# Attention, dense MLP and routed experts on one core: a new order of the attention phase, another float64 decode, a hinted branch

## The chip, the cores and the metric

The kernel runs on one core of one Trainium2 chip. The metric is the device time of one execution in microseconds (us); the median over runs is compared.

## The reference

Three stages follow one another, each over all 1536 tokens (2 batches of 768):

1. Attention with 8 heads of 64: each query sees the keys of the last 96 positions and the first 8 ("global") keys, with a linear distance penalty by head; `n_global` and `n_local` are inputs.

```python
is_global = pos[None, :] < int(n_global)
is_local = (rel >= 0) & (rel < int(n_local))
scores = np.where(keep, scores + bias, -1e9); a = softmax(scores); x = a @ v
```

2. A dense MLP, 512 to 2048 to 512, whose weights `w_in`, `w_out` are float64: `h = x @ w_in; g = max(h, 0) + alpha * min(h, 0); x = g @ w_out`.

3. Eight experts with top-1 routing: `logits = x @ w_gate + modality_bias[modality_id]`, each token goes to its best expert, `relu(x @ w1[e]) @ w2[e]`, scaled by the softmax weight.

## The kernel before

**Precision and tiles.** Every fp32 matmul of the first two stages is three matmuls on values split into a high and a low part. Tokens are cut into 12 tiles of 128; for the MLP two tiles form a block of 256, so there are 6 blocks, and the 16 slices of 128 hidden features are worked in 4 groups of 4.

**Attention of one tile `ti`** (lines 515 to 662): `load_attn` loads `kr`, `qr`, `vr` (256 KB each); `attn_T` transposes k and q on TensorE and splits them into `ring` and `qT`; `attn_S` makes the scores in PSUM (`a`); `attn_P` adds the bias on VectorE (CUSTOM_DVE into `sp`, with the row minimum `mn`) and takes exp on ScalarE; `attn_PT` transposes the probabilities into `pth`; `attn_V` splits v on GpSimd into `vring`; `attn_PV` multiplies and normalises into `x`; `attn_X` transposes `x` into `xT`, the MLP's input.

**MLP step** (lines 1015 to 1053): `step_a` makes `h` (12 matmuls), then ScalarE, VectorE and GpSimd make `t` and the split `g`; `step_b` accumulates `g @ w_out` in `acc`. PSUM holds two banks of `h`.

**Decode of a weight slice** (lines 366 to 383): `load_w` brings 512 KB of raw float64 words (`wraw`); `decode_into` makes fp32 out of the high word `hw` and the top bits of the low word `lw`, into `dx`, and splits it into `w`. There are 32 decodes; the first 10 lie in the attention phase. Before, one decode is: ScalarE Abs; four VectorE instructions (clamp, mask and shift, merge sign, merge low bits); ScalarE Copy; GpSimd subtract.

**What sets the order.** While `plan.on`, instructions are only recorded. `Plan.issue` then simulates the engines with a table of costs and emits the recorded work in the order of simulated starts; among the instructions that could start within `slack` of the earliest, an engine takes the one of the lowest rank, slope times base plus offset by the table `URGENCY` (a kind has two letters at most: L loads of k and q, C constants, D decodes, and so on). There are two such plans: the first covers all of the attention, the first 10 decodes and the MLP steps of blocks 0 to 4 of feature group 0; the second the rest of the MLP up to its last group. The engines run each queue in order; SP issues nearly all loads.

**Between the plans** stands `wide_path` (line 1098): a path for general `n_global` and `n_local` behind a branch that is not taken here. It holds `dense_attention`, unrolled over 8 heads, and a redo of the MLP steps done so far. Every engine loads the flag `fli` (L1099) and branches (L1100); on the way around, each engine adds the semaphore counts that the path would have added and jumps to the join.

`more_constants` (line 476) makes the MLP's `alpha_sb` and the gate's `wg`, `mbs` and `thr`. Line 152 is the recorder, so all recorded instructions bear it, and line 70 is a helper's.

Of the kernel before, what the change touches and what calls it, by code (L numbers as in the profile page):

```python
# [10 lines left out]
F32 = mybir.dt.float32  # L11
# [4 lines left out]
U32 = mybir.dt.uint32  # L16
# [6 lines left out]
P = 128  # L23
# [8 lines left out]
URGENCY = {  # L32
# [6 lines left out]
}  # L39
SLACK = ((63.05, 1544.0), (185.8, math.inf))  # L40


class Plan:
# [9 lines left out]
    }  # L53
    ISSUE, TURN, FIRST, DONE = 500, 1230, 850, 1400

    def __init__(self, tc):
# [210 lines left out]

    def issue(self, rank, slack, ahead):

        self.on = False  # L270
        self.link()
        start = self.simulate(rank, slack, ahead)
        with self.tc.manual_schedule():
            for k in sorted(range(len(self.ops)), key=lambda k: (start[k], k)):
                for call in self.ops[k]["calls"]:
                    call()
        self.ops = []
# [3 lines left out]
def tile_kernel(  # L281
# [51 lines left out]
    def load_attn(ti):  # L333
        b, i = divmod(ti, TPB)
        r = []
        for src, nm in ((k, "kr"), (q, "qr"), (v, "vr")):
            plan.kind = (ti - 1.0, "LV" if nm == "vr" else "L")
            t = ap2.tile([P, H, D], F32, tag=nm, name=nm)
            Y.dma_start(out=t, in_=src[b, :, i * P:(i + 1) * P, :].rearrange("h p d -> p h d"))
            r.append(t)  # L340
        plan.kind = (-2.0, "C")
        raws[ti] = [r[1], r[0], r[2]]
# [23 lines left out]
    def decode_into(t, hi, lo):  # L366
        t = t.rearrange("p k f w -> p (k f) w")
        lw, hw = t[:, :, 0], t[:, :, 1]
        x = decp.tile([P, 512], F32, tag="dx", name="dx")
        S.activation(out=x, in_=hw.bitcast(F32), func=ACTF.Abs)  # L370
        V.tensor_scalar(out=x, in0=x, scalar1=CHI, scalar2=CLO, op0=ALU.min, op1=ALU.max)
        xu = x.bitcast(U32)
        V.tensor_scalar(out=xu, in0=xu, scalar1=0x07FFFFFF, scalar2=3, op0=ALU.bitwise_and, op1=ALU.logical_shift_left)
        V.scalar_tensor_tensor(out=xu, in0=hw, scalar=0xC0000000, in1=xu, op0=ALU.bitwise_and, op1=ALU.bitwise_or)
        V.scalar_tensor_tensor(out=xu, in0=lw, scalar=29, in1=xu, op0=ALU.logical_shift_right, op1=ALU.bitwise_or)
        S.activation(out=hi, in_=x, func=ACTF.Copy)
        G.tensor_tensor(out=lo, in0=x, in1=hi.bitcast(F32), op=ALU.subtract)
# [18 lines left out]
    plan.on = True  # L396
    plan.kind = (-2.0, "C")
    gl = const.tile([P, 4], U32, name="gl")
    Y.dma_start(out=gl[:, 0:2], in_=n_global.bitcast(U32).partition_broadcast(P))
    Y.dma_start(out=gl[:, 2:4], in_=n_local.bitcast(U32).partition_broadcast(P))  # L400
    load_attn(0)
    mraw = const.tile([NTT, P, 2], U32, name="mraw")
    plan.kind = (0.0, "CM")
    Y.dma_start(out=mraw, in_=mod_id.bitcast(U32).rearrange("(t p w) -> t p w", p=P, w=2))
    mrf = const.tile([NF, 2, P], F32, name="mrf")
# [69 lines left out]

    def more_constants():
        nonlocal alpha_sb, mbs, wg, thr
        G.memset(x2[:, :, DM:XW], 0.0)
        wg = const.tile([P, KD, 96], F32, name="wg")
# [8 lines left out]
        T.transpose(mtp[:, 64:64 + NF], mrf[:, 1], ident[0:NF, 0:NF])  # L488
        mf = const.tile([P, 2, NTT], F32, name="mf")
        V.tensor_copy(out=mf[:, 1], in_=mtp[:, 0:NTT])  # L490
        alpha_sb = const.tile([P, NF], F32, name="alpha_sb")
        V.tensor_scalar(out=alpha_sb, in0=mtp[:, 64:64 + NF], scalar1=-1.0, scalar2=1.0, op0=ALU.mult, op1=ALU.add)
# [207 lines left out]
    def dense_attention():  # L700
# [4 lines left out]
        xo = small[:, 400:400 + D]  # L705
        qb = small[:, 480:480 + D]
        vb = flat[:, 7 * SEQ:7 * SEQ + TPB * D].rearrange("p (t d) -> p t d", d=D)
        qt = flat[0:D, 7 * SEQ + TPB * D:7 * SEQ + TPB * D + P]
# [6 lines left out]
        HS = SEQ // 2  # L715
        for h in range(H):
            slope = 2.0 ** -(8.0 * (h + 1) / H)
            with tc.For_i(0, B, 1) as b:
                V.memset(qoff, 0.0)
                with tc.For_i(0, TPB, 1) as i:  # L720
                    for src, dst in ((k, kb), (v, vb)):
                        Y.dma_start(out=dst.unsqueeze(1), in_=src[ds(b, 1), h].rearrange("o (t p) d -> p o t d", p=P))
                    Y.dma_start(out=qb.unsqueeze(1), in_=q[ds(b, 1), h, ds(i * P, P)].rearrange("o p d -> p o d"))
                    pa, pb = bank(ps_a, "a"), bank(ps_a, "a")
# [17 lines left out]

                    V.scalar_tensor_tensor(out=r, in0=r, scalar=-slope, in1=s, op0=ALU.mult, op1=ALU.add)
                    V.tensor_scalar(out=s, in0=s, scalar1=nls[h], scalar2=None, op0=ALU.add)
                    V.tensor_tensor(out=s, in0=s, in1=t1, op=ALU.mult)
# [17 lines left out]
                    V.tensor_scalar(out=xo, in0=pa[:, 0:D], scalar1=sm_, scalar2=None, op0=ALU.mult)  # L763
                    Y.dma_start(out=xgen[ds(b * SEQ + i * P, P), h * D:(h + 1) * D], in_=xo)
                    V.tensor_scalar(out=qoff, in0=qoff, scalar1=float(P), scalar2=None, op0=ALU.add)

    with kind(3.0, "C3"):
        nlsl = const.tile([P, H], F32, name="nlsl")
        for h in range(H):
            V.tensor_scalar(out=nlsl[:, h:h + 1], in0=nl, scalar1=-(2.0 ** -(8.0 * (h + 1) / H)), scalar2=None, op0=ALU.mult)  # L770
    nls = [nlsl[:, h:h + 1] for h in range(H)]

# [319 lines left out]
    LAG = 2  # L1092

    def rank(base, name):
        slope, offset = URGENCY[name]
        return slope * base + offset

    def wide_path(done):
        wide = nc.values_load(fli[0:1, 0:1], min_val=0, max_val=1)  # L1099
        with tc.If(wide > 0, preferred_fallthrough_block=False):  # L1100
            dense_attention()
# [11 lines left out]
            V.memset(x2[:, :, DM:XW], 0.0)  # L1113

    for s_i in range(len(steps) + LAG):
        if s_i < len(steps):
            gi, b, f = steps[s_i]
            if gi == 0 and wp2 is None:
                while f == 0 and b < CB and next(tiles) < (b + 1) * BT - 1:
                    pass  # L1120
                if b == 0 and f == 0:
                    with kind(3.0, "C3"):
                        more_constants()
                if b >= CB and f == 0:
                    for _ in tiles:
                        pass
                    plan.issue(rank, *SLACK[0])
                    wide_path(s_i)
                    at.close()
                    wp2 = p1.enter_context(tc.tile_pool(name="wp2", bufs=GF + 2, side="right", reuse_waits="tile"))  # L1130
                    plan.on = True
            if gi == NF // GF - 1 and b == 0 and f == LAG:
                plan.issue(rank, *SLACK[1])
# [235 lines left out]
```

## Time and profile before

| | us |
|---|---|
| median of 3 runs (lowest, highest) | 608.0 (606.66, 609.71) |
| the profiled execution | 610.72 |
| its span, first to last instruction | 608.9 |
| TensorE matmul (PE) busy | 572.6 (94%) |
| TensorE weight load (PEld) busy | 512.9 (84%) |
| VectorE (DVE) busy | 374.7 (62%) |
| ScalarE (ACT) busy | 309.1 (51%) |
| GpSimd (POOL) busy | 211.0 (35%) |

Busy times are over the whole span, so they hide the stages. The attention phase with its MLP steps reaches from 0 to 162.2 us, where TensorE comes to the branch; the rest of the MLP to about 400; routing and experts to the end. TensorE's busy time is modelled and can hold short gaps. Of the clock that was granted to TensorE the page tells the level: 1.00 is full speed, 0.50 half.

### The profile page before, as it was taken

How to read it: one execution, taken by the hardware profiler on the slowest of the kernel's cores; microseconds unless marked ns; L12 is line 12 of the kernel's file. 1: busy time of each engine (PE TensorE's matmuls, PEld its weight loads, DVE VectorE, ACT ScalarE, POOL GpSimd, SP SyncE). 2: the span in 40 equal slices, each digit the busy share in tenths (PEclk: the TensorE clock that was granted, in tenths of full speed). 3: DMA queues.
4: the chain of work that ended last, by engine and by line, in shares of the span. 5: the costliest groups of instructions: out<-in, count | busy, mean ns of one | idle time of the engine just before them, and what ended most of it. 6: DMA issues, size and time to landing. Idle time of an engine off the chain costs nothing. (4 is left out here: it accounts for less than half of the span.)

```text
span 608.9 us, 13266 instructions
## 1 busy us (share of the span) xinstructions
PE 572.6 (94%) x4572; PEld 512.9 (84%) x4572; DVE 374.7 (62%) x979; ACT 309.1 (51%) x671; POOL 211.0 (35%) x239
## 2 busy tenths in 40 slices
PE   2889999999799999999999999998999999999995
PEld 2778888898688888989998999887889999998994
DVE  6899998686366787775222433878282269972221
ACT  5867887776355444543332333444372268862221
POOL 4835474442146554563322212213012112230110
PEclk9889999999989999999999999999999999999998
DMA  7854569946134332330000000463822399940120
GB/s 191 174 131 134 124 153 163 180 81 104 35 83 127 103 105 71 104 103 1 1 2 0 36 36 36 158 201 94 278 71 62 98 309 363 356 138 34 36 63 26
DMA packets 94384, 69.53 MB, mean 114 GB/s; under 512 B 61883, under 2 KB 82391, under 8 KB 94296
## 3 DMA queue, kind: packets, MB, share of 16 engines
q1 hardware_dynamic: 91736, 60.84, 37.0%
q0 software_dynamic: 2560, 7.64, 4.2%
q8 instruction: 40, 0.66, 0.5%
q14 instruction: 48, 0.39, 0.2%
HBM read 92.88 MB, written 7.30 MB: 165 GB/s over the span
## 5 line engine op out<-in xcount | busy, mean ns | idle before, releaser
L152 PE MATMUL acc<-w,g 128*128 128x512 f32 x432 | 111.1, 404 | 4.9 <-issue 3.9
L152 PE MATMUL h<-xT,w 128*128 128x256 f32 x888 | 114.7, 285 | 0.1
L152 PEld LDWEIGHTS h<-xT,w 128*128 128x128 f32 x888 | 110.8, 190 | 3.3 <-DVE t L152 0.5
L70 PE MATMUL h<-mw,xs 128*128 128x256 f32 x720 | 98.4, 285 | 1.3 <-DVEq L1300 0.7
L152 PEld LDWEIGHTS acc<-w,g 128*128 128x128 f32 x432 | 79.6, 192 | 22.2 <-issue 4.1
L70 PE MATMUL acc<-mw,ht 128*128 128x512 f32 x360 | 97.1, 407 | 0.5 <-DVEq L1300 0.5
L70 PEld LDWEIGHTS h<-mw,xs 128*128 128x128 f32 x720 | 91.3, 189 | 4.7 <-DVEq L1300 1.1
L152 POOL TENSOR_TENSOR g<-t,g 128x256 fp32r<-128x256 f32 x74 | 60.2, 817 | 92.2 <-ACT g L152 62.2
L70 PEld LDWEIGHTS acc<-mw,ht 128*128 128x128 f32 x360 | 63.5, 189 | 12.2 <-DVEq L1300 0.8
L70 POOL DMA_INDIRECT out<-y,sidx x15 | 18.4, 1225 | 146.2 <-DVE y L70 115.9
L152 DVE SCALAR_TENSOR_TENSOR t<-t,alpha_sb,h 128x256 f32<-128x256 f32 x74 | 35.2, 478 | 51.8 <-ACT t L152 49.2
L70 DVE TENSOR_TENSOR mw<-raw,mw 128x1024 fp32r<-128x1024 f32 x48 | 57.8, 1227 | 9.1 <-ACT mw L70 7.4
L152 POOL TENSOR_TENSOR w<-dx,w 128x512 fp32r<-128x512 f32 x32 | 43.4, 1359 | 44.7 <-ACT w L152 42.7
L70 ACT ACTIVATE hs<-h 128x256 f32<-128x256 f32 x60 | 22.9, 381 | 69.3 <-PE h L70 65.3
L152 ACT ACTIVATE t<-h 128x256 f32<-128x256 f32 x74 | 28.1, 380 | 51.9 <-PE h L152 50.4
L70 DVE TENSOR_TENSOR ht<-a,ht 128x256 fp32r<-128x256 f32 x60 | 25.3, 422 | 47.0 <-ACT ht L70 46.9
L70 ACT ACTIVATE mw<-raw 128x1024 fp32r<-128x1024 f32 x48 | 49.4, 1055 | 6.5 <-DMA raw<-in_moe_w 2.4
L152 DVE SCALAR_TENSOR_TENSOR dx<-wraw,dx 128x512 uint32<-128x512 uint32 x64 | 50.9, 799 | 0.5
L152 ACT ACTIVATE sp<-sp,mn 128x256 f32<-128x256 f32 (+1 forms) x96 | 39.8, 480 | 11.1 <-DVE mn L152 10.9
L152 ACT ACTIVATE g<-t 128x256 fp32r<-128x256 f32 x74 | 30.8, 417 | 26.7 <-DVE t L152 21.7
L70 POOL TENSOR_TENSOR g<-t,g 128x256 fp32r<-128x256 f32 x22 | 17.9, 815 | 58.6 <-ACT g L70 58.5
L70 PE MATMUL acc<-w,g 128*128 128x512 f32 x144 | 38.0, 400 | 0.0
(168 smaller groups left out, 851.9 us busy)
## 6 DMA issues: line engine op xcount, KB each, us to landing
raw<-in_moe_w SPq DMA_DIRECT2D x117, 512.0 KB
wraw<-in_moe_w_in SPq DMA_DIRECT2D x16, 512.0 KB
wraw<-in_moe_w_out SPq DMA_DIRECT2D x16, 512.0 KB
xs<-x SPq DMA_DIRECT2D x12, 258.0 KB
kr<-in_k SPq DMA_DIRECT2D x12, 256.0 KB
qr<-in_q SPq DMA_DIRECT2D x12, 256.0 KB
vr<-in_v SPq DMA_DIRECT2D x12, 256.0 KB
vring<-vglob SPq DMA_DIRECT2D x8, 96.5 KB
```

The costliest lines, as they stand in the source:

```text
L70: return method(*a, **kw)
L152: call = lambda: method(*a, **kw)
```

## The change

- **Start.** The kinds of tile 0's k and q get a rank below everything (base -1e6), the two scalars `gl` come next; `mraw` is no longer loaded among them.
- **Decode.** ScalarE takes Abs scaled by 65536 and, new, Sign in place over `hw`. The clamp and, new, the multiplication by the sign go to GpSimd in the first plan and to VectorE behind it. VectorE shifts `lw` in place and merges: in the first plan two instructions for four.
- **Constants.** `alpha_constants` stays in the first plan; `gate_constants` (`wg`, `mbs`, the modality's transpose, the memset of `x2`'s last columns) goes into the second.
- **Branch.** The flag is loaded inside the first plan, ahead of work whose simulated start lies within `LEAD` of the end, and TensorE gets a prefetch hint for the branch there. The general path now stands right behind the branch, with the way around last.
- **General attention** loops over heads in the program in place of 8 unrolled copies; the eight `nlsl` constants go. On ScalarE the rows between branch and join fall from about 180 to about 80.
- **Tables.** `URGENCY` and the first `SLACK` have new numbers, so all of the first plan is in a new order.

```diff
-    "A": (0.02, 228.0), "B": (0.06921, 81.0), "C": (16.99, -57.0), "C1": (17.59, 5.0),
+    "A": (95.73, -22.0), "B": (100.0, 46.0), "C": (0.7547, -17.0), "C1": (0.7079, -94.0),
...
-SLACK = ((63.05, 1544.0), (185.8, math.inf))
+SLACK = ((57.46, 1710.0), (185.8, math.inf))
...
+    LEAD = 8000
...
-    def issue(self, rank, slack, ahead):
+    def issue(self, rank, slack, ahead, late=None):
...
+                if late and start[k] > max(start) - self.LEAD:
+                    late()
+                    late = None
...
-            plan.kind = (ti - 1.0, "LV" if nm == "vr" else "L")
+            plan.kind = (ti - 1.0 if ti or nm == "vr" else -1e6, "LV" if nm == "vr" else "L")
...
+        eng = G if plan.on and wp2 is None else V
-        S.activation(out=x, in_=hw.bitcast(F32), func=ACTF.Abs)
-        V.tensor_scalar(out=x, in0=x, scalar1=CHI, scalar2=CLO, op0=ALU.min, op1=ALU.max)
+        S.activation(out=x, in_=hw.bitcast(F32), func=ACTF.Abs, scale=65536.0)
+        S.activation(out=hw.bitcast(F32), in_=hw.bitcast(F32), func=ACTF.Sign)
+        eng.tensor_scalar(out=x, in0=x, scalar1=CHI * 65536.0, scalar2=CLO * 65536.0, op0=ALU.min, op1=ALU.max)
         xu = x.bitcast(U32)
-        V.tensor_scalar(out=xu, in0=xu, scalar1=0x07FFFFFF, scalar2=3, op0=ALU.bitwise_and, op1=ALU.logical_shift_left)
-        V.scalar_tensor_tensor(out=xu, in0=hw, scalar=0xC0000000, in1=xu, op0=ALU.bitwise_and, op1=ALU.bitwise_or)
-        V.scalar_tensor_tensor(out=xu, in0=lw, scalar=29, in1=xu, op0=ALU.logical_shift_right, op1=ALU.bitwise_or)
+        V.tensor_scalar(out=lw, in0=lw, scalar1=29, scalar2=None, op0=ALU.logical_shift_right)
+        V.scalar_tensor_tensor(out=xu, in0=xu, scalar=3, in1=lw, op0=ALU.logical_shift_left, op1=ALU.bitwise_or)
+        eng.tensor_tensor(out=x, in0=x, in1=hw.bitcast(F32), op=ALU.mult)
         S.activation(out=hi, in_=x, func=ACTF.Copy)
         G.tensor_tensor(out=lo, in0=x, in1=hi.bitcast(F32), op=ALU.subtract)
...
-    plan.kind = (-2.0, "C")
+    plan.kind = (-5e5, "C")
     gl = const.tile([P, 4], U32, name="gl")
...
-        for h in range(H):
-            slope = 2.0 ** -(8.0 * (h + 1) / H)
+        with tc.For_i(0, H, 1) as h:
...
+    def wide_flag():
+        wide.append(nc.values_load(fli[0:1, 0:1], min_val=0, max_val=1))
+        tc.mark_branch_hint_location("wide", hint=wide[0], engines=EN_PE)
+
     def wide_path(done):
-        wide = nc.values_load(fli[0:1, 0:1], min_val=0, max_val=1)
-        with tc.If(wide > 0, preferred_fallthrough_block=False):
+        with tc.If(wide[0] > 0, label="wide"):
...
-                        more_constants()
+                        alpha_constants()
...
-                    plan.issue(rank, *SLACK[0])
+                    plan.issue(rank, *SLACK[0], wide_flag)
                     wide_path(s_i)
...
+                    with kind(40.0, "L2"):
+                        gate_constants()
```

The order of instructions at three places follows. First SP, which issues the loads, at the start of the program; before:

```order
L152 DMA gl<-in_n_global 128x2
L152 DMA gl<-in_n_local 128x2
L152 DMA wraw<-in_moe_w_in 128x4x256
L152 DMA wraw<-in_moe_w_out 128x1024
L152 DMA kr<-in_k 128x8x64
L152 DMA qr<-in_q 128x8x64
L152 DMA kr<-in_k 128x8x64
L152 DMA qr<-in_q 128x8x64
L152 DMA vr<-in_v 128x8x64
L1099 TENSOR_LOAD fli
```

and in the changed kernel:

```order
L154 DMA kr<-in_k 128x8x64
L154 DMA qr<-in_q 128x8x64
L154 DMA gl<-in_n_global 128x2
L154 DMA gl<-in_n_local 128x2
L154 DMA wraw<-in_moe_w_in 128x4x256
L154 DMA wraw<-in_moe_w_out 128x1024
L154 DMA mrf<-in_moe_alpha 16x128
L154 DMA vr<-in_v 128x8x64 x2
L154 DMA kr<-in_k 128x8x64
L154 DMA qr<-in_q 128x8x64
```

Tile 0's k and q went from behind two weight loads to the front; tile 1's went behind two loads of v; SP's load of the flag left this place.

Second, GpSimd (POOL) where the first weights are decoded, with tile numbers; before, behind the constants:

```order
L152 COPY fscr<-fscr 128x128
L152 TENSOR_TENSOR w_229<-dx,w_229 128x512
L152 TENSOR_SCALAR vring_126<-vr 128x8x64
L152 TENSOR_TENSOR vr<-vr,vring_126 128x512
L152 TENSOR_SCALAR vring_126<-vr 128x512
L152 TENSOR_TENSOR vring_126<-vr,vring_126 128x512
```

and in the changed kernel (`dx<-dx` is the clamp, `dx<-dx,wraw` the multiplication by the sign):

```order
L154 TENSOR_SCALAR dx<-dx 128x512
L154 COPY fscr<-fscr 128x32
L154 TENSOR_SCALAR vring_125<-vr 128x8x64
L154 COPY fscr<-fscr 128x128
L154 TENSOR_TENSOR vr<-vr,vring_125 128x512
L154 TENSOR_SCALAR vring_126<-vr 128x8x64
L154 TENSOR_SCALAR vring_125<-vr 128x512
...
L154 TENSOR_TENSOR dx<-dx,wraw 128x512
L154 TENSOR_TENSOR vring_126<-vr,vring_126 128x512
L154 TENSOR_TENSOR w_222<-dx,w_222 128x512
```

One GpSimd instruction of a decode became three, among the splits of v.

Third, TensorE (PE) in front of the branch; before:

```order
L152 MATMUL h<-xT,w_258 128x256 x12
L152 MATMUL a<-ident,x 128x128 x4
L1099 TENSOR_LOAD fli
L1100 COMPARE_AND_BRANCH
L1100 UNCONDITIONAL_BRANCH
```

and in the changed kernel (the left out rows are the last tile's `attn_PV`):

```order
L154 MATMUL h<-xT,w_240 128x256 x12
L1115 TENSOR_LOAD fli
L1385 BRANCH_PREFETCH_HINT
L154 MATMUL acc<-w_225,g 128x512 x6
L154 MATMUL h<-xT,w_251 128x256 x12
...
L154 MATMUL acc<-w_234,g 128x512 x6
L154 MATMUL a<-ident,x 128x128 x4
L1119 COMPARE_AND_BRANCH
```

The flag's load and the hint moved ahead of 24 MLP matmuls, `attn_PV` and the last transposes; the branch now stands right behind those transposes, whose copy is ScalarE's last work there too.

## Rows read from the trace of the kernel before

**Rows 1.** Busy us of each engine by stretch (instructions), clock, DMA share, GB/s.

```profile
core 0: us, PE busy (x) PEld busy (x) DVE busy (x) ACT busy (x) POOL busy (x), PEclk, DMA share, GB/s
0.00:20.00 20.00, 8.42 (x62) 6.81 (x63) 14.34 (x61) 12.58 (x33) 11.47 (x30) 1.00 0.85 187
20.00:100.00 80.00, 73.69 (x953) 65.38 (x948) 76.06 (x253) 61.57 (x133) 44.60 (x49) 0.96 0.62 138
100.00:162.00 62.00, 60.54 (x752) 53.42 (x750) 41.01 (x122) 39.36 (x85) 24.70 (x31) 1.00 0.69 122
166.00:380.00 214.00, 212.85 (x1358) 192.69 (x1359) 117.30 (x252) 89.49 (x210) 86.18 (x93) 0.99 0.18 58
```

**Rows 2.** Timeline of the start: start us, length us, instruction, idle time before.

```profile
1.29 0.42 SPq L152 DMA_DIRECT2D gl<-in_n_local  x1
...
5.53 0.24 DVE L152 TENSOR_SCALAR gparts<-gl 128x2 uint32<-128x2 uint32 x2 [1.49 <-DMA gl<-in_n_local]
...
10.10 1.09 PE L152 MATMUL a<-ident,kr 128*128 128x128 f32 x4 [10.10 <-DMA kr<-in_k]
...
15.01 0.29 DVE L152 CUSTOM_DVE_ANT_0 sp<-a,bias 128x128 f32<-128x128 f32 x1
...
16.18 1.11 PE L152 MATMUL a<-ident,kr 128*128 128x128 f32 x4
...
18.47 0.65 PE L152 MATMUL a<-ident,qr 128*128 128x128 f32 x4 [0.32 <-PE a L152]
```

**Rows 3.** The view of Rows 1, of four short stretches.

```profile
4.00:16.00 12.00, 5.09 (x32) 4.17 (x32) 9.15 (x48) 7.56 (x21) 4.39 (x8) 1.00 1.08 261
24.00:30.00 6.00, 5.85 (x72) 5.28 (x70) 5.16 (x21) 5.23 (x12) 3.97 (x6) 0.72 0.60 130
34.00:40.00 6.00, 4.79 (x65) 4.41 (x63) 5.69 (x23) 4.92 (x11) 1.82 (x3) 0.72 0.30 91
164.00:172.00 8.00, 5.90 (x15) 4.74 (x16) 4.03 (x8) 2.21 (x4) 0.03 (x1) 0.58 0.11 19
```

**Rows 4.** TensorE's waits, 20 to 100 us: total us, times, longest.

```profile
PE a L152 <- DVE pth L152: 1.8, 3, 1.2
PE a L152 <- DVE x L152: 1.4, 2, 1.2
```

**Rows 5.** Groups on VectorE, 20 to 100 us: the decodes (busy us, mean ns).

```profile
L152 DVE SCALAR_TENSOR_TENSOR dx<-wraw,dx 128x512 uint32<-128x512 uint32 x15 | 10.3, 684 | 0.1
...
L152 DVE TENSOR_SCALAR dx<-dx 128x512 f32<-128x512 f32 x8 | 4.4, 555 | 0.0
...
L152 DVE TENSOR_SCALAR dx<-dx 128x512 uint32<-128x512 uint32 x8 | 3.3, 418 | 0.0
```

**Rows 6.** Groups on GpSimd, 20 to 100 us, of the same size.

```profile
L152 POOL TENSOR_TENSOR w<-dx,w 128x512 fp32r<-128x512 f32 x8 | 10.9, 1361 | 21.7 <-ACT w L152 21.7
L152 POOL TENSOR_SCALAR vring<-vr 128x512 bf16<-128x512 f32 x15 | 10.4, 691 | 10.9 <-PE a L152 9.7 <-DMA vr<-in_v 0.6
```

**Rows 7.** Instructions that write `dx`, whole span: ns least/median/most.

```profile
L152 DVE TENSOR_SCALAR dx<-dx x64: 397/426/1131, 8.3 to 277.2; 128x512 f32<-128x512 f32 x32, 128x512 uint32<-128x512 uint32 x32
L152 DVE SCALAR_TENSOR_TENSOR dx<-wraw,dx x64: 649/687/1667, 9.3 to 280.8; 128x512 uint32<-128x512 uint32 x64
L152 ACT ACTIVATE dx<-wraw x32: 646/666/707, 7.4 to 274.3; 128x512 f32<-128x512 f32 x32
```

**Rows 8.** Timeline around the branch, columns as in Rows 2.

```profile
161.62 0.60 PE L152 MATMUL a<-ident,x 128*128 128x128 f32 x4
...
162.25 0.60 ACT L152 ACTIVATE xT<-a 128x512 fp32r<-128x512 f32 x1
...
166.10 1.22 PE L152 MATMUL acc<-w,g 128*128 128x512 f32 x2 [3.89 <-issue]
166.75 0.67 ACT L152 ACTIVATE dx<-wraw 128x512 f32<-128x512 f32 x1 [3.52 <-issue]
```

**Rows 9.** Instructions of the branch, line 1100: ns least/median/most, first to last start.

```profile
L1100 PEldq COMPARE_BRANCH  x2: 95/1866/3638, 161.8 to 162.4; - x2
```

More of the change, by code (lines that the diff above doesn't have):

```diff
@@ L400, in tile_kernel @@
     Y.dma_start(out=gl[:, 2:4], in_=n_local.bitcast(U32).partition_broadcast(P))
+    plan.kind = (-2.0, "C")
     load_attn(0)
-    mraw = const.tile([NTT, P, 2], U32, name="mraw")
     plan.kind = (0.0, "CM")
-    Y.dma_start(out=mraw, in_=mod_id.bitcast(U32).rearrange("(t p w) -> t p w", p=P, w=2))
     mrf = const.tile([NF, 2, P], F32, name="mrf")
@@ L474, in tile_kernel, with alpha_constants, gate_constants @@
     alpha_sb = mbs = wg = thr = None
-    def more_constants():
-        nonlocal alpha_sb, mbs, wg, thr
+    def alpha_constants():
+        nonlocal alpha_sb
+        mtp = bank(ps_a, "a")
+        T.transpose(mtp[:, 0:NF], mrf[:, 1], ident[0:NF, 0:NF])
+        alpha_sb = const.tile([P, NF], F32, name="alpha_sb")
+        V.tensor_scalar(out=alpha_sb, in0=mtp[:, 0:NF], scalar1=-1.0, scalar2=1.0, op0=ALU.mult, op1=ALU.add)
+    def gate_constants():
+        nonlocal mbs, wg, thr
         G.memset(x2[:, :, DM:XW], 0.0)
+        mraw = const.tile([NTT, P, 2], U32, name="mraw")
+        Y.dma_start(out=mraw, in_=mod_id.bitcast(U32).rearrange("(t p w) -> t p w", p=P, w=2))
         wg = const.tile([P, KD, 96], F32, name="wg")
@@ L487, in more_constants @@
         T.transpose(mtp[:, 0:NTT], mrf[0:NTT, 0], ident[0:NTT, 0:NTT])
-        T.transpose(mtp[:, 64:64 + NF], mrf[:, 1], ident[0:NF, 0:NF])
         mf = const.tile([P, 2, NTT], F32, name="mf")
         V.tensor_copy(out=mf[:, 1], in_=mtp[:, 0:NTT])
-        alpha_sb = const.tile([P, NF], F32, name="alpha_sb")
-        V.tensor_scalar(out=alpha_sb, in0=mtp[:, 64:64 + NF], scalar1=-1.0, scalar2=1.0, op0=ALU.mult, op1=ALU.add)
         V.tensor_scalar(out=mf[:, 0], in0=mf[:, 1], scalar1=-1.0, scalar2=1.0, op0=ALU.mult, op1=ALU.add)
@@ L706, in dense_attention @@
         qb = small[:, 480:480 + D]
+        slope, nls = small[:, 3:4], small[:, 4:5]
         vb = flat[:, 7 * SEQ:7 * SEQ + TPB * D].rearrange("p (t d) -> p t d", d=D)
@@ L715, in dense_attention @@
         HS = SEQ // 2
-        for h in range(H):
-            slope = 2.0 ** -(8.0 * (h + 1) / H)
+        step = 2.0 ** -(8.0 / H)
+        V.memset(slope, -step)
+        V.tensor_scalar(out=nls, in0=nl, scalar1=-step, scalar2=None, op0=ALU.mult)
+        with tc.For_i(0, H, 1) as h:
             with tc.For_i(0, B, 1) as b:
@@ L721, in dense_attention @@
                     for src, dst in ((k, kb), (v, vb)):
-                        Y.dma_start(out=dst.unsqueeze(1), in_=src[ds(b, 1), h].rearrange("o (t p) d -> p o t d", p=P))
-                    Y.dma_start(out=qb.unsqueeze(1), in_=q[ds(b, 1), h, ds(i * P, P)].rearrange("o p d -> p o d"))
+                        Y.dma_start(out=dst.unsqueeze(1).unsqueeze(1), in_=src[ds(b, 1), ds(h, 1)].rearrange("o u (t p) d -> p o u t d", p=P))
+                    Y.dma_start(out=qb.unsqueeze(1).unsqueeze(1), in_=q[ds(b, 1), ds(h, 1), ds(i * P, P)].rearrange("o u p d -> p o u d"))
                     pa, pb = bank(ps_a, "a"), bank(ps_a, "a")
@@ L741, in dense_attention @@
                     V.tensor_tensor(out=lo, in0=lo, in1=t1, op=ALU.add)
-                    V.scalar_tensor_tensor(out=r, in0=r, scalar=-slope, in1=s, op0=ALU.mult, op1=ALU.add)
-                    V.tensor_scalar(out=s, in0=s, scalar1=nls[h], scalar2=None, op0=ALU.add)
+                    V.scalar_tensor_tensor(out=r, in0=r, scalar=slope, in1=s, op0=ALU.mult, op1=ALU.add)
+                    V.tensor_scalar(out=s, in0=s, scalar1=nls, scalar2=None, op0=ALU.add)
                     V.tensor_tensor(out=s, in0=s, in1=t1, op=ALU.mult)
@@ L763, in dense_attention @@
                     V.tensor_scalar(out=xo, in0=pa[:, 0:D], scalar1=sm_, scalar2=None, op0=ALU.mult)
-                    Y.dma_start(out=xgen[ds(b * SEQ + i * P, P), h * D:(h + 1) * D], in_=xo)
+                    Y.dma_start(out=xgen[ds(b * SEQ + i * P, P), ds(h * D, D)], in_=xo)
                     V.tensor_scalar(out=qoff, in0=qoff, scalar1=float(P), scalar2=None, op0=ALU.add)
[L767 to L771, printed above, removed]
+            V.tensor_scalar(out=slope, in0=slope, scalar1=step, scalar2=None, op0=ALU.mult)
+            V.tensor_scalar(out=nls, in0=nls, scalar1=step, scalar2=None, op0=ALU.mult)
     QW = FE // 4
@@ L1092, in tile_kernel @@
     LAG = 2
+    wide = []
+    EN_PE = [getattr(mybir.EngineType, n) for n in ("PE",)]
     def rank(base, name):
```

1 line of the change is left out of this document (removed), and 8 rows, old and new, of the table URGENCY.

## The prediction, made before the changed kernel was run

> **What bounds the kernel now.** I read the busy time by stretch first, then the clock in short stretches, the start, the waits of TensorE, and last the branch.
>
> From 166 to 380 us TensorE is busy 212.85 of 214 us, while VectorE has 117 and ScalarE 89 [rows 1]: nothing in that stretch is to be had by faster decodes, and nothing is lost by somewhat slower ones. What the change can move lies ahead of it, in the attention phase and at the branch, and there the profile shows three losses.
>
> The start: TensorE's first work begins at 10.10 us, when tile 0's k has come [rows 2]. From 20 to 100 us VectorE is busy 76.06 of 80 us and TensorE 73.69; VectorE is the fuller one, and of TensorE's 6.3 us of idle time the two largest waits, 1.8 and 1.4 us, are for VectorE's `pth` and `x` [rows 1, 4]. In the same stretch the granted clock is 0.72 on average from 24 to 30 and from 34 to 40 us [rows 3]: with the levels 1.00 and 0.50 that is 0.56 of 6 us at half speed, 3.4 us each, so 1.7 us of work lost each, 3.4 together. Both follow on stretches in which TensorE waited.
>
> The branch: TensorE ends the last transposes at 162.2 and starts again at 166.10, an idle time of 3.89 us that no engine's semaphore explains [rows 8]; one of its two branch instructions lasted 3638 ns [rows 9]. Then the clock is 0.58 on average over 164 to 172 us [rows 3], that is 0.84 of 8 us, 6.7 us, at half speed. About 0.8 of them fall into the idle time; the other 6 cost 3.0 us of work. The branch is worth up to 3.9 + 3.0 = 6.9 us.
>
> **The start, part by part.** k goes to the place of the first scalar load. The second scalar was issued at 1.29 and used at 5.53, 4.24 us later [rows 2]; k, issued at 0.83 at the head of the queue, should likewise begin to land at about 5.1, and its 0.26 MB take 1.0 us at the 261 GB/s of 4 to 16 us [rows 3]. TensorE starts between 5.1 and 6.1; I take 5.6, 4.5 us earlier. The scalars fall behind 0.5 MB, 2 us by that rate, so VectorE's mask chain begins near 7.5 in place of 5.53, and the first bias is ready near 10.5, still ahead of the 15.01 at which it is first used [rows 2]. Tile 1 limits the lead: its k now lies behind 2.1 MB (tile 0's k and q, two weight loads, two loads of v), so with its own 0.26 MB it lands at 4 + 2.36/0.261 = 13.0 us and q at 14.0, where TensorE took them at 16.18 and 18.47 [rows 2]. That is a lead of 3.2 to 4.5. I count -4.0, between -1.0 (the lead is eaten by VectorE, below) and -4.6.
>
> **The decodes.** Ten lie in the first plan, eight of them between 20 and 100 us. Eight cost VectorE 10.3 + 4.4 + 3.3 = 18.0 us [rows 5], 2.25 each. Two instructions stay: a merge at 0.684, and a shift over strided words that the trace does not show, between the 0.418 of the old shift and the 0.684 of a two-input instruction [rows 5]; I take 0.45, because it has one input. That leaves 1.13, so VectorE sheds 1.1 us a decode, 11 in all. The moved constants of the gate and the eight `nlsl`, some 15 instructions, are small and not counted. ScalarE gets Sign, like Abs 0.67 us [rows 7], 6.7 us in ten, beside 18 us of its own slack from 20 to 100 [rows 1]: nothing. GpSimd gets a clamp and a multiplication, 0.69 and 1.36 us by the same size in [rows 6], 20.5 us in ten decodes; it was busy 44.6 of 80 us [rows 1] and stays under 80%, and weights are decoded well ahead of their use.
>
> What does TensorE get of VectorE's 11 us? At most its idle 6.3 and the lost 3.4 us from 20 to 100, 9.7. At least nothing, or a loss if GpSimd's instructions hold VectorE up: the same shapes on VectorE last up to 1131 and 1667 ns at a median of 426 and 687 [rows 7]. The new order has other waits, since its chain from scores over exp to `pth` is as long as before. I count -4.0, rather less than half of 9.7, since I named VectorE as the releaser for 3.2 of the 6.3 us only and since the lead of the start must pass through the same VectorE. The range is -9.7 to +6.
>
> [...]
>
> **The branch.** TensorE loads the flag (0.5 us in its queue) and gets the hint behind 12 `h` matmuls, and between hint and branch stand 12 `acc` and 12 `h` matmuls, the 40 small ones of an `attn_PV` and 4 transposes, over 5 us of work, more than the 3.64 of the slow branch. If the fetch then runs beside this work, 3.9 us of idle time go. What is late next is ScalarE: the first matmul behind the join waits until ScalarE has passed its own branch, and in the new order ScalarE's last instruction is the copy of those last transposes. It follows them by some 0.2 us, lasts 0.60 [rows 8], and with its branch TensorE resumes about 1.3 us after its transposes: -2.6. After so short a pause I expect the clock to stay: -3.0. ScalarE waited 3.52 us behind its branch too [rows 8]; its path around is now under half as long, so I expect that wait gone. But it must then do four decode instructions of 0.67 in place of two before its copies of `acc`, and TensorE, no longer at half speed, comes sooner to the third `h`, whose bank is free only after ScalarE and VectorE. I give back 1.3 us, two Signs. The sum is -4.3, between 0 (below) and -6.9.
>
> **At nothing.** The gate's constants, 2 fills on GpSimd and some 6 small VectorE instructions, go into the second plan, and the 22 decodes there keep four VectorE instructions (clamp and multiplication on VectorE) and gain 0.67 on ScalarE, 14.7 us: all beside a TensorE that is full [rows 1]. If that cover failed, the 0.67 before a late decode would show as a wait for `w`. The head loop runs in no part of this execution.
>
> **The sum.** -4.0 - 4.0 - 4.3 = -12.3. Against the profiled execution's 610.72 (span 608.9, 1.8 around it) that is 598.4; that execution lay 2.7 above the median of 608.0, and from the median it is 595.7. I forecast 596, its own range 590 to 602.
>
> **The rivals.**
> - *The jump still stalls.* The hint may name the wrong side (it is fed by the flag's value, which is 0 here) or do nothing; the way around lies far behind the branch for TensorE as before. No row shows a hint at work, and the 3638 ns stay. Then only 8.0 us come: 600. [...]
> - *The lead is eaten.* Loads, not TensorE, set the first 20 us (the DMA share is 0.85 there and 1.08 from 4 to 16 us [rows 1, 3]), and the same bytes come in any order: the start gives -1.0, and with VectorE's chain unchanged the decodes give -2.0. With the branch 7.3: 601. Against it: tile 1's k and q are wanted later than they land.
> - *GpSimd becomes the bound (slower).* Every one of the 20 new instructions holds VectorE: +20.5 - 11 = +9.5 in a stretch that VectorE fills, and two more cold stretches of 1.7, +3.4; less 4.0 and 4.3 it is +4.6: 613. It turns slower only once over 19 of the 20.5 us block VectorE. Before, 15 two-input instructions lost next to nothing in the mean (684 ns against a median of 687 [rows 5, 7]), which speaks against it.
> - *All of it comes.* TensorE runs full from 5.6 us on: -4.5 - 9.7 - 6.9 = -21: 587.
>
> **How the numbers follow.** Forecast 0.50, the stalled jump 0.15, the eaten lead 0.17, GpSimd 0.06, all of it 0.12. The range 587 to 605 holds these but GpSimd's case, half of the best one, and the upper tails of the two at 600 and 601. About half a per cent, 3 us, is what a measurement of this kernel tells from no change: faster means below 605, slower above 611. The forecast and the best case are faster whole; of the two near 600 about a fifth (0.07) ends at 605 or above. Faster 0.87, same 0.07, slower 0.06.
>
> **What would show it.** Right: TensorE's first transposes near 5.6 us; tile 1's near 13 to 14; VectorE from 20 to 100 us well under 95% with waits on `pth` and `x` smaller; no stretch at half clock behind the branch, a pause of about 1.3 us, and a branch instruction of TensorE near 0.1 us; TensorE at the branch by about 154. Wrong: a branch of 3.6 us again; VectorE instructions on `dx` or `pth` of 1 us and more in number; waits of TensorE for `vring`, `w` or `g` from a late GpSimd; any new idle time of TensorE from 166 to 380.

## The result, and the profile after

The changed kernel takes 600.98 us (median of 4 runs, 599.01 to 603.01), the kernel before 608.86 beside it: a ratio of 0.9858, 95% interval [0.9814, 0.9902], or 7.9 us less. Measured again (experiment 9) the ratio was 0.9886 [0.9857, 0.9916], the medians 6.5 us apart. The forecast was 596. The execution profiled first took 599.01 and is the fastest of its four, so its 11.7 us less than the profiled 610.72 flatter the change.

The busy time by stretch, in the columns of [rows 1]:

```profile
core 0: us, PE busy (x) PEld busy (x) DVE busy (x) ACT busy (x) POOL busy (x), PEclk, DMA share, GB/s
0.00:20.00 20.00, 10.15 (x61) 7.52 (x62) 10.19 (x47) 12.86 (x33) 10.48 (x30) 1.00 0.79 172
20.00:100.00 80.00, 75.74 (x1010) 67.15 (x1008) 73.16 (x240) 69.48 (x152) 62.86 (x68) 1.00 0.66 155
166.00:380.00 214.00, 213.72 (x1394) 194.74 (x1395) 119.50 (x303) 99.89 (x233) 88.14 (x94) 1.00 0.20 62
24.00:30.00 6.00, 5.34 (x77) 4.17 (x78) 5.40 (x20) 5.90 (x15) 4.38 (x6) 1.00 0.74 190
34.00:40.00 6.00, 5.33 (x69) 4.32 (x69) 5.80 (x22) 6.00 (x14) 3.70 (x6) 1.00 0.46 137
```

TensorE issues 1010 matmuls between 20 and 100 us where it issued 953 [rows 1], while VectorE is busy 73 us instead of 76 and GpSimd 63 instead of 45. The two half-clock stretches of [rows 3] are gone in this execution.

The start, in the columns of [rows 2]:

```profile
0.82 0.45 SPq L154 DMA_DIRECT2D kr<-in_k  x1
...
4.33 1.09 PE L154 MATMUL a<-ident,kr 128*128 128x128 f32 x4 [4.33 <-DMA kr<-in_k]
...
7.39 0.24 DVE L154 TENSOR_SCALAR gparts<-gl 128x2 uint32<-128x2 uint32 x2 [3.35 <-DMA gl<-in_n_local]
...
7.74 0.68 DVE L154 TENSOR_TENSOR ring<-a,ring 128x512 fp32r<-128x512 f32 x1
...
11.56 0.28 DVE L154 CUSTOM_DVE_ANT_0 sp<-a,bias 128x128 f32<-128x128 f32 x1
...
14.13 1.09 PE L154 MATMUL a<-ident,kr 128*128 128x128 f32 x4 [0.44 <-DMA kr<-in_k]
...
15.79 1.11 PE L154 MATMUL a<-ident,qr 128*128 128x128 f32 x4 [0.57 <-DVE pth L154]
...
19.27 1.14 PE L154 MATMUL a<-vring,pth 128*128 128x64 bf16 x18 [1.99 <-POOL vring L154]
```

A lead of 5.8 us at TensorE's first work (4.33 against 10.10 [rows 2]) is 3.5 at VectorE's first work on the scores (11.56 against 15.01), since VectorE must wait for the scalars (`gl`) and only then touches tile 0's k (`ring`). At tile 1's q it is 2.7.

TensorE's waits from 20 to 100 us (total us, times, longest), and the decode's groups on VectorE and GpSimd there:

```profile
PE a L154 <- DVE mn L154: 1.3, 2, 0.8
PE h L154 <- DVE t L154: 0.9, 1, 0.9
PE a L154 <- DVE x L154: 0.6, 2, 0.5
PE a L154 <- DVE pth L154: 0.4, 1, 0.4
```

```profile
L154 DVE SCALAR_TENSOR_TENSOR dx<-dx,wraw 128x512 uint32<-128x512 uint32 x9 | 6.1, 683 | 0.2
...
L154 DVE TENSOR_SCALAR wraw<-wraw 128x512 uint32<-128x512 uint32 x9 | 4.6, 521 | 0.0
```

```profile
L154 POOL TENSOR_TENSOR dx<-dx,wraw 128x512 f32<-128x512 f32 x10 | 14.0, 1404 | 9.5 <-DVE dx L154 7.4 <-ACT t L154 2.0
...
L154 POOL TENSOR_SCALAR dx<-dx 128x512 f32<-128x512 f32 x9 | 5.7, 633 | 3.8 <-ACT dx L154 3.6
```

The waits on `pth` and `x` fell from 3.2 us [rows 4] to 1.0. VectorE's share of a decode is 0.68 + 0.52 = 1.20 us; GpSimd's new one 2.04.

The branch, which [rows 8] show of before, and its instructions (now line 1119), as in [rows 9]:

```profile
156.77 0.60 PE L154 MATMUL a<-ident,x 128*128 128x128 f32 x4
160.06 3.01 PE L154 MATMUL acc<-w,g 128*128 128x512 f32 x12 [2.69 <-ACTq L1119]
```

```profile
L1119 PEldq COMPARE_BRANCH  x1: 803/803/803, 156.4 to 156.4; - x1
...
L1119 ACTq COMPARE_BRANCH  x1: 50/50/50, 157.4 to 157.4; - x1
L1119 DVEq COMPARE_BRANCH  x1: 72/72/72, 158.0 to 158.0; - x1
L1119 ACTq EVENT_SEMAPHORE  x1: 17/17/17, 160.0 to 160.0; - x1
L1119 DVEq EVENT_SEMAPHORE  x1: 21/21/21, 160.9 to 160.9; - x1
```

TensorE is at the branch 4.8 us sooner (157.4 against 162.2). Its own branch instruction is down from 3638 to 803 ns, and yet it stands still for 2.69 us: it now waits for an event of ScalarE, which comes 2.6 us after ScalarE's own branch, though that branch is counted with 50 ns. VectorE has the same gap, 2.9 us.

In the kernel before, ScalarE's event stood elsewhere:

```profile
L1100 ACTq COMPARE_BRANCH  x2: 38/42/45, 163.4 to 163.5; - x2
...
L1100 ACTq EVENT_SEMAPHORE  x1: 17/17/17, 163.4 to 163.4; - x1
```

It came at 163.4, between the branch and the jump to the join, so ScalarE's long way to its next work (166.75 [rows 8]) lay behind the event and hid beside TensorE's own 3638 ns. In the new layout the way around stands last, the one branch is itself the far jump, and the event comes behind it. By these rows, the wait that TensorE now has comes from the layout too, not only from the length of ScalarE's jump.

### The profile page after: what moved, and what is told of

It reads as the page before. It is cut to its first block, busy times and chain, and to the rows that moved or that the text cites. A ratio compares the mean times of both kernels' runs of the same rounds, so it can differ in the third digit from the quotient of the medians.

```text
span 597.2 us, 13277 instructions
## 1 busy us (share of the span) xinstructions
PE 568.7 (95%) x4572; PEld 509.9 (85%) x4572; DVE 363.9 (61%) x951; ACT 327.2 (55%) x703; POOL 228.0 (38%) x259
## 5 line engine op out<-in xcount | busy, mean ns | idle before, releaser
L154 PEld LDWEIGHTS h<-xT,w 128*128 128x128 f32 x888 | 111.4, 189 | 5.4 <-DVE t L154 1.9
L154 PEld LDWEIGHTS acc<-w,g 128*128 128x128 f32 x432 | 77.5, 188 | 17.6 <-ACTq L1119 2.9
L72 PEld LDWEIGHTS acc<-mw,ht 128*128 128x128 f32 x360 | 63.5, 188 | 12.3 <-DVEq L1320 1.3
L72 PEld LDWEIGHTS h<-xT,w 128*128 128x128 f32 x264 | 34.5, 191 | 1.8
```

What stands on the lines that cost most here:

```text
L72: return method(*a, **kw)
L154: call = lambda: method(*a, **kw)
```

## The experiments

Twelve kernels ran. My theory after the first profile was that the start's lead is eaten by 20 us, that the decode and the branch carry the gain, and that each engine's own jump sets the pause. The first half of it fell. All ratios are to the kernel before on the same chip; 0.01 is 6.1 us. A difference from the changed kernel is given as a range, by its two ratios, 0.9858 and 0.9886.

**1. Without the hint.**

```
-        tc.mark_branch_hint_location("wide", hint=wide[0], engines=EN_PE)
```

> The changed kernel without the branch hint on TensorE; the flag is still loaded early and the blocks stand as in the changed kernel. Theory: the hint alone took TensorE's branch from 3638 to 803 ns, so without it a branch instruction of TensorE of about 3.6 us is back, the pause at the branch is 3.5 to 3.9 us in place of 2.69, a half-clock stretch of 6 to 7 us follows it, and the time is 1 to 4 us above the changed kernel's (600.98): 602 to 605. Rival: the early load and the new layout shortened the branch; then the pause stays at 2.7 us, the clock stays full, and the time is 601.

600.83 us, ratio 0.9876 [0.9845, 0.9907]: no slower. Branch instructions and TensorE's next work in this run:

```profile
L1118 PEldq COMPARE_BRANCH  x1: 3572/3572/3572, 157.6 to 157.6; - x1
...
L1118 ACTq COMPARE_BRANCH  x1: 50/50/50, 158.7 to 158.7; - x1
...
L1118 ACTq EVENT_SEMAPHORE  x1: 17/17/17, 161.3 to 161.3; - x1
```

```profile
161.41 4.30 PE L154 MATMUL acc<-w,g 128*128 128x512 f32 x12 [2.78 <-ACTq L1118]
```

TensorE's slow branch is back, but it ends at the same moment as ScalarE's jump (161.3), so the pause is 2.78 us as with the hint. The hint shortens TensorE's branch (3572 ns without it, 803 with it in the first profile), and with ScalarE's jump as long as that (2.6 us in both) it is worth nothing.

**2. The hint on ScalarE and VectorE as well.**

```
-    EN_PE = [getattr(mybir.EngineType, n) for n in ("PE",)]
+    EN_PE = [getattr(mybir.EngineType, n) for n in ("PE", "Activation", "DVE")]
```

> The changed kernel with the same hint on ScalarE and VectorE as well as on TensorE. Theory: the 2.6 us between ScalarE's branch (157.4) and its next event (160.0), and VectorE's 2.9 us, are fetches of their own branch targets, and they are what TensorE waits for; with hints both fall below 1 us, TensorE's pause falls from 2.69 to 1.0 to 1.4 us, and the time by 1 to 2 us, to about 599.5. Rival: ScalarE and VectorE wait there for something else (an event of another engine at the join), and the pause stays at 2.7 us and the time at 601.

600.34 us, ratio 0.9874 [0.9845, 0.9903]; pause 2.82 us. The rows of ScalarE:

```profile
L1119 ACTq COMPARE_BRANCH  x1: 73/73/73, 157.8 to 157.8; - x1
...
L1119 ACTq EVENT_SEMAPHORE  x1: 17/17/17, 160.5 to 160.5; - x1
```

2.7 us, as without. Either the gap doesn't hang on what the engine jumps over, or this hint doesn't shorten it on ScalarE; experiment 8 tells the two apart.

**3. The old decode.** The changed kernel with the old `decode_into`; the planner orders it anew.

> The changed kernel with the decode of the kernel before (four VectorE instructions, no Sign, nothing more on GpSimd); its order is worked out anew by the same table. Theory: the new decode gives VectorE about 1.1 us a decode and TensorE some 2 to 5 us of them; VectorE's busy time from 20 to 100 us is back above 75 of 80 us and GpSimd's near 45, TensorE is at the branch 2 to 5 us after 157.4, and the time is 603 to 606. Rival: what VectorE sheds comes back as waits for GpSimd's two longer instructions, and the time stays within 1 us of 601 or falls.

605.9 us, ratio 0.9964 [0.9941, 0.9987]: 4.7 to 6.4 us slower than the changed kernel, as the theory had it.

```profile
20.00:100.00 80.00, 73.22 (x935) 64.30 (x935) 74.85 (x237) 60.48 (x133) 44.86 (x50) 0.98 0.54 137
```

VectorE is back at 75 us, TensorE at 935 matmuls. The last transposes before the branch end at 162.2, where they ended before the change, although the first work began 5.7 us sooner (4.43 against 10.10). In this one execution the early start was gone by the branch; in time the kernel is still 1.7 us below the kernel before (605.9 against 607.61, medians).

**4. k and q in their old rank.**

```
-            plan.kind = (ti - 1.0 if ti or nm == "vr" else -1e6, "LV" if nm == "vr" else "L")
+            plan.kind = (ti - 1.0, "LV" if nm == "vr" else "L")
-    plan.kind = (-5e5, "C")
+    plan.kind = (-2.0, "C")
```

> The changed kernel with k and q of tile 0 back in their old place behind the scalar loads. Theory: the 5.8 us by which TensorE's first work came earlier were given back by 20 us, since ScalarE's bias and GpSimd's split of v come no sooner; TensorE starts near 10 us, is at the branch within 1 us of 157.4, and the time is 600 to 602. Rival: the early start is a real lead of 3 to 4 us, as predicted; then the branch is reached at about 161 and the time is 604 to 605.

616.0 us, ratio 1.0142 [1.0111, 1.0173], which neither theory had. It isn't a clean undoing: under the new table the planner put the first two weights, both scalars, alpha and two loads of v ahead of tile 0's k, the first scores were reached 9 us later (20.70), and TensorE waited 8.7 us for `sp`. It says how dear a late start can be, not what this one was worth.

**5. k and q behind the scalars and two weights, every other order held.**

```
+            if late:
+                loads = [k for k in seq if self.ops[k]["code"] == "S"][:6]
+                for k in loads[:2]:
+                    seq.remove(k)
+                at = seq.index(loads[5]) + 1
+                seq[at:at] = loads[:2]
```

> The changed kernel in its own order on every engine, except that the loads of tile 0's k and q are issued behind the two scalar loads and the first two weight loads, as at the head of the kernel before. (The run with the old start before it let the planner work out a new order, which put k and q behind nine loads; this one holds the order.) Theory: the loads at the head carry most of the gain; tile 0's k lands near 10 us, TensorE's first work comes 5 to 6 us later, the first scores, which had been reached at 11.56, come near 15, and the branch is reached 2 to 4 us later than 157.4: 603 to 605. Rival: the lead is given back by 20 us, as ScalarE's bias and GpSimd's split of v set the pace; branch within 1 us of 157.4, time 600 to 602.

(In experiment 4 it was seven loads, not nine.)

603.86 us, ratio 0.9914 [0.9893, 0.9935]: 1.7 to 3.4 us slower than the changed kernel. First work at 9.92, first scores at 15.60, last transposes before the branch ended at 161.27, 3.9 us later than in the first profile and 3.0 later than in that of experiment 9. So the early loads are worth something to this order, and my theory of their loss was wrong.

**6. Clamp and multiplication on VectorE, in the same places.**

```
-        eng = G if plan.on and wp2 is None else V
+        eng = plan.engine(nc.vector, "G") if plan.on and wp2 is None else V
```

> The changed kernel in its own order, except that in the first plan the clamp and the multiplication of the decode run on VectorE, in the places where GpSimd had them. Theory: VectorE, at 73 of 80 us from 20 to 100, has no room for 8 times 1.1 us; it becomes full (78 or more), TensorE waits for it, the branch is reached 3 to 7 us later, and the time is 604 to 608, like the 605.9 with the old decode in an order of its own. Rival: the loss with the old decode came from the new order, not from VectorE's load; then the time stays within 2 us of 601.

608.56 us, ratio 1.0001 [0.9981, 1.0022], 7.0 to 8.7 us slower.

```profile
20.00:100.00 80.00, 71.17 (x922) 62.54 (x921) 75.37 (x238) 63.34 (x136) 43.09 (x47) 0.98 0.57 137
```

```profile
PE a L154 <- DVE x L154: 2.8, 6, 0.9
PE a L154 <- DVE mn L154: 2.5, 3, 1.3
```

What GpSimd took over is what VectorE can't carry without TensorE waiting for it. The theory had VectorE at 78 us or more and the time at 608 at most; VectorE is at 75.4, and the time is higher. Why it loses more than experiment 3 wasn't tried; its order was made for a lighter VectorE, that of experiment 3 for its own.

**7. The branch's part alone, in the kernel before** (early flag, hint, one branch instead of two; its own order and decode).

```
-        wide = nc.values_load(fli[0:1, 0:1], min_val=0, max_val=1)
-        with tc.If(wide > 0, preferred_fallthrough_block=False):
+        with tc.If(wide[0] > 0, label="wide"):
```

> The kernel before with the branch's part of the change alone: the flag loaded 8 us early, the hint on TensorE, and the new layout with one branch where there were two. Theory: TensorE's pause falls from 3.89 to 2.7 to 2.9 us, since ScalarE's own jump ends it now; the half-clock stretch behind it comes or stays away by chance, and the time falls by 1 to 2 us: 606 to 607. Rival: the branch was worth its predicted 4.3 us and more; the clock stays full and the time is 603 to 604.

608.39 us, ratio 0.9999 [0.9977, 1.0022]: nothing, even less than the theory had.

```profile
159.25 0.60 PE L154 MATMUL a<-ident,x 128*128 128x128 f32 x4
163.92 4.47 PE L154 MATMUL acc<-w,g 128*128 128x512 f32 x12 [4.07 <-ACTq L1112]
```

TensorE's branch fell to 1043 ns, but ScalarE in that order has a `t` and a `g` to do beside the last copy, jumps at 160.4 and is there at 163.9: its event lies behind its jump here too, 3.4 us after the branch. No run keeps the old two branches together with the hint, so what the hint alone would give in the old layout stays open.

This profile also shows how far one execution of the kernel before can be trusted. Up to the branch it has the order of the kernel before, apart from the flag's loads, and its last transposes end at 159.85 where the first profile had 162.22; its clock from 20 to 100 us was 0.98 on average, against 0.96 [rows 1]. So a time of arrival at the branch that is taken from one profile can't carry a difference of 2 us.

**8. A short body.** The general attention and the catching up behind it are left out; one tile's transposes and copies stay.

```
-            dense_attention()
-            for ti in range(NTT):
...
-            for z in steps[:done]:
...
+            x = decp.tile([P, H, D], F32, tag="dx", name="xw")
+            V.memset(x, 0.0)
+            attn_X(0, (x[:, 0:4], x[:, 4:8]))
```

> The changed kernel with the body of the branch cut to one tile's transposes and their copies; the general attention and the catching up behind it are left out (they run in no execution shown here). Some of the last transposes and their copies then stand behind the join. Theory: the 2.6 to 2.9 us that ScalarE and VectorE take from their branch to the next event are fetches of instructions far away; with the target near, each engine is behind its branch within 0.5 us, TensorE's pause is under 1 us, no half-clock stretch follows, and the time falls by 2 to 5 us, to 596 to 599. Rival: the events at the join cost that time whatever the distance; the pause stays above 2 us and the time at 600 to 601.

597.09 us, ratio 0.9809 [0.9781, 0.9836], and no half clock behind the branch (1.00 from 160 to 220 us).

```profile
L1119 PEldq COMPARE_BRANCH  x1: 264/264/264, 155.2 to 155.2; - x1
L1119 ACTq COMPARE_BRANCH  x1: 55/55/55, 155.4 to 155.4; - x1
...
L1119 ACTq EVENT_SEMAPHORE  x1: 17/17/17, 155.9 to 155.9; - x1
L1119 DVEq COMPARE_BRANCH  x1: 72/72/72, 156.1 to 156.1; - x1
L1119 DVEq EVENT_SEMAPHORE  x1: 21/21/21, 156.7 to 156.7; - x1
```

0.5 and 0.6 us in place of 2.6 and 2.9: the gap goes with the length of the body, not with the join, and the jump with what follows it costs this kernel 3.0 to 4.7 us. What an engine does in the gap isn't shown. In the changed kernel's first profile two DMA queues of the kind `instruction` carried three packets from 157.4 to 160.0, ScalarE's gap, and nothing else moved (queue, kind: packets, MB, share):

```profile
q8 instruction: 1, 0.02, 3.5%
q14 instruction: 2, 0.02, 2.3%
```

Which engine a packet was for, and whether an engine waited for it, the profile doesn't say.

**9. The changed kernel again.**

> The changed kernel itself, beside the three edits of it that follow. Expected by every theory: 600 to 602 in the median, with runs between 599 and 603. What the profile tells apart: if the half-clock stretch behind the branch was taken away by the change, as predicted, none is seen here either; if it comes and goes behind a pause of 2.6 to 3.1 us, one of 3 to 7 us can be seen here, with the same pause, the same order, and 1 to 3 us more.

601.64 us, ratio 0.9886 [0.9857, 0.9916]. The profile has the same order and a pause of 2.79 us, and behind it

```profile
160.00:168.00 8.00, 6.96 (x34) 6.12 (x35) 4.78 (x9) 4.92 (x9) 1.83 (x3) 0.79 0.22 58
```

a clock of 0.79 on average; with the levels 1.00 and 0.50, which the trace before shows (0.50 from 166 to 172 us), that is 0.42 of 8 us = 3.4 us at half speed. In the first profile it was 1.00. The half clock wasn't removed; it stayed away once.

The mean clock that is on record for every execution tells what the clock is worth here. In the executions with a mean clock of 0.991 to 0.994 the kernel before took 607.2 us in the mean (19 of the 51 that ran beside the experiments), the changed kernel 601.5 (6 of its 10): 5.7 us of the gain are there at the same mean clock. Over all of them the difference is 7.0, so some 1.3 us came with a clock that was higher on average (0.992 against 0.989); in which stretch, these means don't say.

**10. The last copy on VectorE.**

```
-        S.activation(out=xT[:, 0, :, c], in_=xp, func=ACTF.Copy)
+        if plan.on and ti == NTT - 1:
+            plan.engine(nc.vector, "A").tensor_copy(out=xT[:, 0, :, c], in_=xp)
+        else:
+            S.activation(out=xT[:, 0, :, c], in_=xp, func=ACTF.Copy)
```

> The changed kernel in its own order, except that the copy of the last transposes before the branch, ScalarE's last instruction there, runs on VectorE. Theory: ScalarE's jump (2.6 us from its branch) ends TensorE's pause; without the copy ScalarE is at its branch at about 155.7 and behind it at about 158.4, so that TensorE's pause falls from 2.7 to 1.0 to 1.4 us; VectorE jumps some 0.7 us later than before, beside TensorE's 3 us of acc matmuls, and may make the h matmuls behind them wait up to 1 us. The time falls by 1 to 2.5 us, to 598.5 to 600. Rival: VectorE's jump, later by its second copy, takes ScalarE's place, and the pause before acc or before h adds up to the same 2.7 us; the time stays at 601.

600.66 us, ratio 0.9872 [0.9844, 0.9901]: the rival.

```profile
158.99 3.02 PE L154 MATMUL acc<-w,g 128*128 128x512 f32 x12 [0.70 <-ACTq L1122]
...
162.30 1.10 DVE L154 TENSOR_SCALAR dx<-dx 128x512 f32<-128x512 f32 x2 [2.55 <-DVEq L1122]
...
166.72 0.47 DVE L154 SCALAR_TENSOR_TENSOR t<-t,alpha_sb,h 128x256 f32<-128x256 f32 x1
167.25 2.14 PE L154 MATMUL h<-xT,w 128*128 128x256 f32 x9 [2.07 <-DVE t L154]
```

The pause falls to 0.70 us as worked out, and 2.07 come back 8 us later: VectorE leaves its jump at 162.0, does eight decode instructions, and only then the `t` that frees the bank of the third `h`. 0.70 + 2.07 is 2.77.

**11. Two swaps at the start** (GpSimd ends tile 0's split of v first; ScalarE copies tile 1's k ahead of seven of eight bias instructions).

```
+                behind([split[1 + 1], split[4]], split[5])
+                behind([ring], bias[0])
+                behind(bias[4:], qT)
```

> The changed kernel with two swaps in the order of its first 20 us: GpSimd finishes the split of tile 0's v before it begins tile 1's, and ScalarE makes tile 1's ring copy behind the first of the eight bias instructions and four of the eight behind tile 1's qT. Theory: the part of the start's lead that was lost (5.8 us at TensorE's first work, 3.9 at the branch) was lost to these two orders; TensorE's wait of 2.0 us for vring falls to 0.5 or less, tile 1's first score matmul comes at 19 to 20 in place of 21.24, the branch is reached 1 to 2 us before 157.4 and the time is 599 to 600. Rival: the lead is lost to VectorE further on, as its 73 of 80 us suggest; then the wait for vring goes, another takes its place before 60 us, and the time stays at 601.

601.21 us, ratio 0.9881 [0.9852, 0.9911]: no gain. The wait for `vring` fell from 2.0 to 0.8 us, but in this execution

```profile
9.36 0.24 DVE L154 TENSOR_SCALAR gparts<-gl 128x2 uint32<-128x2 uint32 x2 [5.32 <-DMA gl<-in_n_local]
9.71 0.68 DVE L154 TENSOR_TENSOR ring<-a,ring 128x512 fp32r<-128x512 f32 x1
```

the scalars were used at 9.36 instead of 7.39, and the first big block of scores began 2.0 us later (11.45 against 9.48). By this profile alone it stays open whether the swaps gave nothing or were covered by the late scalars.

**12. Both edits.**

> The changed kernel with the copy on VectorE and the two swaps at the start together. Theory: the two edits lie 130 us apart and add up: 1 to 2.5 us and 1 to 2 us, 596.5 to 599. Rival: neither moves anything, 601.

601.03 us, ratio 0.9875 [0.9844, 0.9906]: nothing, the rival. Here the scalars were used at 7.88, as in experiment 9 (7.93), the wait for `vring` was 0.8 us, and the last transposes ended at 158.22, where they ended in experiment 9 (158.25): the swaps bring nothing that reaches the branch. At the branch the pause was 0.68 us, and 2.1 us came back at the third `h`, as in experiment 10. No version that keeps the general attention beat the changed kernel.

## Why the prediction was right in direction and 5 us too low

**Start, −4.0: right in kind, 1.7 to 3.4 measured.** First work came at 4.33 (5.6 was forecast), the mask chain began at 7.39 (7.5), tile 1's k was transposed at 14.13 (13.0). What was missed: I checked that the bias is ready before the time of its *old* first use, not that VectorE, in order, had tile 0's `ring` queued behind the scalars. That cost about 2 us of the lead at 8 us, and the use of `gl` varies (5.68 at the head of the queue in experiment 5; between 7.06 and 9.36, in experiments 6 and 11, behind k and q).

**Decodes, −4.0: right, 4.7 to 6.4 measured.** VectorE's rest is 1.20 us for 1.13 forecast, and its two waits in [rows 4] shrank as expected. The forecast had TensorE at the branch at 154, some 8 us before 162.2; it came at 158.3 (experiment 9) or 157.4, so the two parts together moved it by 3.9 to 4.8 us, and against the 159.9 of experiment 7 by 1.6 to 2.5. With the decode alone (experiment 5) it came at 161.3, with the start alone (experiment 3) at 162.2. That looks as if each part needed the other, but these are single executions, and the times don't bear it out: beside the kernel before, the medians fall by 1.7 us with the start alone, by 4.3 with the decode alone, and by 6.5 to 7.9 with both. The two nearly add.

The third rival, GpSimd as the bound, is out: it had 613 us, VectorE's merge stayed at 683 ns, against 684 before [rows 5], and with the clamp and the multiplication on VectorE the kernel is slower (experiment 6). GpSimd's own multiplication took 1404 ns in the mean, 1287 at least, and VectorE's new shift 521 in the mean from 20 to 100 us, against a median of 422 over the whole span. That each of the 20 new instructions holds VectorE for its whole length, the 20.5 us of this rival, was a supposition that no run shows; in its place VectorE's busy time from 20 to 100 us fell from 76.06 [rows 1] to 73.16 us. Which of the longer instructions waited for the other engine the trace doesn't say.

**Branch, −4.3: this step failed.** It held three claims.
- *"3.9 us of idle time go ... about 1.3 us after its transposes: -2.6."* The pause went from 3.89 to 2.7–2.8. I wrote of ScalarE's 3.52 us "I expect that wait gone" because its way around was under half as long. It isn't gone, it is 2.6 us, and since ScalarE's event now stands behind it, TensorE waits for it. Removing TensorE's stall (3572 to 803 ns) moved nothing (experiments 1 and 7); a shorter body does (experiment 8: gaps of 0.5 and 0.6 us, 3.0 to 4.7 us in time).
- *"After so short a pause I expect the clock to stay: -3.0."* The pause wasn't short, and behind it the clock differs from execution to execution: from 2.6 to 3.2 us of pause, the profiles show 0 (first), 3.4 (experiments 1, 3, 4, 6, 9) and 6.8 us (2, 5, 11) at half speed; behind none (8), 0. Before the change it was 6.7, in experiment 7 3.4 behind 4.07.
- *The price of the branch alone:* 0 in the kernel before (experiment 7, within 1.4 us). What the early flag and the single branch are worth inside the changed kernel was not tried; only the hint was taken out there (experiment 1: nothing).

The first rival, the stalled jump, gave the right time (600) by luck: its condition, that TensorE's 3638 ns stay, did not hold (803), and another engine's jump took its place. That the slow branch waits for a fetch was my reading and was not shown; the runs show how long it is without the hint (3572 ns in experiment 1), and that ScalarE's and VectorE's gaps are 0.5 and 0.6 us with a short body (experiment 8).

**At nothing: held, with a small gain.** From 166 to 380 us TensorE has 0.3 us of idle time, against 1.15 [rows 1], in the first profile; none of the 22 later decodes shows as a wait for `w`. That of 180 to 260 us, 1.0 us before and 1.2 in experiment 7, is 0 in the profiles of the changed kernel and of experiments 3 and 5; which part of the change took it away was not tried apart.

**The sum.** The forecast had 12.3, and 6.5 to 7.9 were measured. Start and decode were forecast at 8.0 together and carry nearly all of what came (1.7 and 4.3 alone, by the medians above); the branch, forecast at 4.3, gives nothing alone. These figures hold for a kernel with the new table of ranks, the moved constants and the new branch, which are in every one of these runs but experiment 7; the shares of the table and the constants were not taken apart, and an order made for other parts can cost more than the part (experiments 4 and 6).

Worked out again from the profile of experiment 9, against that of before: at the branch 3.9 us sooner, pause 1.1 less, 1.0 less behind it, half clock 3.4 us less = 1.7 of work. That is 7.7 of the 8.3 us between the two spans (608.9 and 600.6). Against the profile of experiment 7, with the same 3.4 us of half clock behind its pause, it is 1.6 us sooner, 1.3 less pause and 1.2 less behind it: 4.1 of the 4.7 us between the spans (605.3 and 600.6). The shorter pause belongs to the new order, in which ScalarE has only the copy left to do there.

## What to carry to other kernels

When a stall of one engine at a join is to go, list when every engine passes that join, in the trace and with its own jump, and whether the event that the others wait for comes ahead of that jump or behind it: the next one in the list is the gain's limit, and an engine with a short way around can be it. Don't conclude from one profile how two parts of a change work together; compare the medians with one, the other and both. When loads change places, follow the first instruction on each in-order engine that stands behind the load that moved back. Before a clock effect is counted as a gain, profile the same kernel twice, and compare executions at the same mean clock.

## What the runs showed of the hardware that was not expected

A branch counted with 50 to 84 ns can still cost its engine 2.5 (ScalarE, experiment 4) to 3.2 us (VectorE, experiment 5), and 3.4 to 3.6 with the longer body of experiment 7: on TensorE the wait stands inside the branch instruction (3572 ns, experiment 1), on ScalarE and VectorE between it and the next event. A hint (6.5 us ahead of the branch in the first profile) shortened TensorE's to between 483 and 1043 ns in most runs, to 1392 and 1769 in experiments 4 and 3, and left ScalarE's at 2.7 us (experiment 2). And the same order of instructions with the same pause (2.69 and 2.79 us) was followed by no half clock in one execution (the first profile) and by 3.4 us of it in another (experiment 9).
